# Decode attention with a gated MLP: x loaded as 16 rows, the last values in two halves, 76 first key rows

## The chip, the cores and the metric

The kernel runs on one core of a Trainium2 chip. The metric is the device time of one execution in microseconds (us). A core has a matrix engine (PE, its weight loads shown apart as PEld), a vector engine (DVE), a scalar engine (ACT), GpSimd (POOL) and SyncE (SP), which here only issues transfers. ACT and SP each have a queue of transfers; all transfers run on the same 16 DMA engines. Matmuls read SBUF and write PSUM.

## The reference

One token, x of 512 values. It is normalised (xn), and goes two ways: through attention over the last 4096 positions of a cache of 32 heads, and through a small MLP. The results are multiplied and added to x.

```
xn = layernorm(x)
q = (xn @ wq) in 32 heads of 128
k, v = the last 4096 rows of k_cache, v_cache of each head      # bf16, 32 MiB each
s = softmax(q k^T / sqrt(128)) v, all heads side by side, @ wo  # wo: 4096 x 512
h = gelu(layernorm(xn) @ w1); hs = shift(h) @ w2                # S = 1: the shifted h is zero
x1 = xn + hs
g = silu(x1 + gelu(layernorm(x1) @ w3) @ w4)
out = x + s * g
```

With a sequence of one position, the shifts by one and two positions leave only padding, so the kernel multiplies w2 by a column of zeros (`shifted_bf`) and doesn't load w1.

## The kernel before

**Groups.** The 32 heads are taken in 8 groups of 4 (G = 4, NG = 8). Keys of a group are one tile of 128 partitions by 128 rows ("chunks", CP = 128) of 128 values, 4 MiB; partition p holds 128 neighbouring positions of one head (32 partitions a head). Values lie the same way. The K tiles have three buffers and the V tiles two (K_BUFS, V_BUFS), and the V buffers take the place of the first weights (pool `wts`), once those have been used.

**Loads.** All but x and wq are issued by SP, in program order (`load`, L75): w2, w3, w4, then K0 in two halves, K1, K2, V0, K3, V1 and so on, with pieces of wo between them; at the end V7 in three pieces (`cuts`, L528: chunks 0 to 64, 64 to 96, 96 to 128), and four rows of wo of 128 x 512, two by two (L544). A buffer's next load waits for the engines that read the buffer, and what stands behind it in SP's queue waits too. ACT issues x twice and wq (L78 to L85): as 128 partitions of four values (`x_bf`, from which the statistics and q are made) and as four rows of 128 values on partitions 0, 32, 64 and 96 (`x_row`, for the end), after POOL has cleared that tile.

**Start.** The statistics of x (`ln_stats`), the product with wq in rows (L208), copies of q for DVE (`q_bc`) and for PE (`q_pair`), and the MLP (L245 to L280), whose result g_row waits for the end. This part is in an order that a scheduler makes; from L529 on the order of PE, DVE and ACT is the program's own.

**Scores.** The keys' rows of a group are shared out. For the first nd(g) rows of each partition (L308: 64 for group 0 and from LATE = 7 on, else 80) DVE multiplies by q and sums over 128 values (`k_vector`, L321 and L323), in four steps of nd/4 rows. The others go to PE: transposes of pairs of rows (`k_turn`, L339), a copy by ACT (L342), and two matmuls per pair (`k_scores`, L350), in batches of up to eight rows; `sm_own` (L359) takes the right head's part. `sm_max`, `sm_turn`, `sm_exp`, `sm_den`, `sm_rden` make the softmax. In round s of the loop (L533) the scores of group s are made, the softmax of group s-1, and the values of group s-2 (LAG = 2).

**Values.** `v_wide` (L427) multiplies four chunks by the probabilities of four chunks at a time, 16 rows into the sum `ov`; `v_turn` transposes it, `v_add` (L450) takes the fitting parts together to `oT`, and `v_out` (L471) multiplies by 1/denominator to `o`. For the last group the first 96 chunks go that way; `v_add` writes its result over a PSUM tile that `v_open` has opened, and `v_part` (L461) then adds the last 32 chunks to that tile one by one with the values as weights, so that nothing has to be turned.

**End.** `ox_spread` and `ox_pick` turn blocks of o for the wide products with wo (`y_wide`, L520), summed over four partitions by `rows_add` (L155). The last four heads go head by head (`y_head`, `rows_add`): four matmuls each with one row of wo into y_ps. Then y = y_ps * g_row, out_row = y + x_row (L654, L656), and the store. `warm(n)` (L509) issues n matmuls of zeros that no one reads.

`small.tile([P, 96], BF16, name="pad")` at L71 is not used by anything: it only moves what lies behind it.

Of the kernel before, what the change touches and what calls it, by code (L numbers as in the profile page):

```python
# [18 lines left out]
G = 4  # L19
# [3 lines left out]
LATE = 7  # L23
# [3 lines left out]
def kernel(  # L27
# [24 lines left out]
    CP = G * W // P  # L52
    PB = P // G
# [14 lines left out]
    ps_o = ctx.enter_context(tc.tile_pool(name="ps_o", bufs=1, space=PSUM))  # L68
    ps_y = ctx.enter_context(tc.tile_pool(name="ps_y", bufs=1, space=PSUM))
    sm_pool = ctx.enter_context(tc.tile_pool(name="sm", bufs=3))  # L70
    small.tile([P, 96], BF16, name="pad")  # L71
    wts_guard = tc.tile_pool(name="wts", bufs=1)
    wts = wts_guard.__enter__()

    def load(dst, src):  # L75
        return tc.keep_in_program_order(nc.sync.dma_start(out=dst, in_=src))  # L76

    x_bf = small.tile([P, KC], BF16, name="x_bf")  # L78
    nc.scalar.dma_start(out=x_bf[:], in_=A_x.rearrange("a b (p c) -> p (a b c)", p=P))
    x_row = small.tile([P, P], BF16, name="x_row")  # L80
    nc.gpsimd.memset(x_row[:], 0.0)
    nc.scalar.dma_start(out=x_row[0:P:32, :], in_=A_x.rearrange("a b (j n) -> (a b j) n", j=KC))
    wq_sb = wts.tile([P, KC, HD], BF16, name="wq_sb")
    nc.scalar.dma_start(out=wq_sb[:].rearrange("p c n -> p (c n)"),
                        in_=A_wq.rearrange("(a b c) n -> b a (c n)", a=4, c=KC))  # L85
# [93 lines left out]
        return xc, negmean, rstd  # L179


    x_f = small.tile([P, KC], FP32, name="x_f")
    nc.vector.tensor_copy(out=x_f[:], in_=x_bf[:])
    xc, negmean, rstd = ln_stats(x_f[:], "x")
    xn_f = small.tile([P, KC], FP32, name="xn_f")
    nc.vector.tensor_scalar(out=xn_f[:], in0=xc[:], scalar1=rstd[:], scalar2=None, op0=ALU.mult)
# [51 lines left out]
    z3_bf = small.tile([P, KC], BF16, name="z3_bf")  # L238
    nc.vector.tensor_scalar(out=z3_bf[:], in0=xc3[:], scalar1=rstd3[:], scalar2=None, op0=ALU.mult)

    xn_row = small.tile([P, P], FP32, name="xn_row")
    nc.vector.tensor_scalar(out=xn_row[:], in0=x_row[:], scalar1=negmean[:], scalar2=rstd[:],
                            op0=ALU.add, op1=ALU.mult)
# [62 lines left out]
    st = {}  # L306

    def nd(g):  # L308
        return 64 if g == 0 or g >= LATE else 80

    def k_open(g):
        st[g] = {
# [132 lines left out]

    def v_add(g):
        s = st[g]
        if g < NG - 1:
            s["oT"] = sm_pool.tile([P, G], FP32, tag="oT", name="oT")
        nc.vector.tensor_reduce(out=s["oT"][:], in_=s["ot"][:].rearrange("p (x m) -> p m x", m=32)[:, 0:G, :],  # L450
                                axis=AX.X, op=ALU.add)

    def v_open(g):
        st[g]["oT"] = ps_tr.tile([P, G], FP32, tag="pt", name="oT")
        nc.tensor.matmul(st[g]["oT"][:], lhsT=zero_bf[:], rhs=zero_bf[:, 0:G], start=True, stop=False,
                         skip_group_check=True)

    def v_part(g, v, c0, c1):
        s = st[g]
        for c in range(c0, c1):  # L460
            nc.tensor.matmul(s["oT"][:], lhsT=v[:, c, :], rhs=s["pT"][:, c, :], start=False,  # L461
                             stop=(c == CP - 1), skip_group_check=True)

    def v_out(g):
        h = G * g
        b = [i for i, (h0, _) in enumerate(blocks) if h >= h0][-1]
        if b not in o_blk:
            o_blk[b] = sm_pool.tile([P, blocks[b][1]], BF16, tag=f"o{b}", bufs=1, name="o")
        c = h - blocks[b][0]
        if g >= NG - 5:  # L470
            nc.vector.tensor_tensor(out=o_blk[b][:, c:c + G], in0=st[g]["oT"][:], in1=st[g]["rden"][:],  # L471
                                    op=ALU.mult)
            return
        for k in range(G):
            nc.scalar.mul(o_blk[b][:, c + k:c + k + 1], st[g]["oT"][:, k:k + 1], st[g]["rden"][:, k:k + 1])
# [49 lines left out]
        rows_add(y_ps, o_blk[3][:, h - h_part:h - h_part + 1], wo_row(h), h == H - 1)  # L525

    NG = H // G
    cuts = (0, 64, 96, CP)  # L528
    region = tc.manual_schedule(engines={mybir.EngineType.PE, mybir.EngineType.DVE,  # L529
                                         mybir.EngineType.Activation})  # L530
    region.__enter__()
# [1 line left out]
    for s in range(NG + LAG):  # L533
# [7 lines left out]
            wo_rows = v_pool.tile([P, H - h_part, D], BF16, tag="wo_rows", bufs=1, name="wo_rows")  # L541
        if last:
            v = load_kv(v_pool, A_v_cache, h, cuts)
            for r in (H - G, H - 2):  # L544
                load_rows(r, 2)
        elif h >= 0:
            v = load_kv(v_pool, A_v_cache, h)
        if h == 3:
# [71 lines left out]
        elif s == NG:  # L620
            ox_pick(1)
            sm_turn(NG - 1)
            sm_exp(NG - 1)
            y_wide(1, False)
            sm_den(NG - 2)
            sm_rden(NG - 2)
            y_wide(0, False)
            warm(3)
            v_wide(h, v)
            sm_den(NG - 1)  # L630
            sm_rden(NG - 1)
            v_turn(h)
            v_add(h)
            v_out(h)
            ox_spread(2)
        else:
            v_open(h)
            warm(2)
            v_wide(h, v, cuts[1], last=False)
            ox_pick(2, 1)  # L640
            y_wide(2, True)
            nc.scalar.copy(out=y_sum[:], in_=yr[0][:].rearrange("p j n -> p (j n)"))
            v_wide(h, v, cuts[2], cuts[1])
            warm(2)
            v_turn(h)
            v_add(h)
            rows_add(y_ps, ind, y_sum, False)
            v_part(h, v, cuts[2], CP)
            v_out(h)
            for r in range(H - G, H):  # L650
                y_head(r)
# [36 lines left out]
```

## Time and profile before

| | us |
|---|---|
| median of 3 runs | 193.54 (193.43 to 193.62) |
| the profiled execution | 193.37 |
| its span, first to last instruction | 191.2 |
| x_bf issued, landed | 0.74, 4.76 |
| first DVE work on K0 | 25.93 |
| K1 landed | 41.98 |
| last values landed | 186.19 |
| store issued | 188.71 |

Bytes moved: 79.02 MB, 413 GB/s over the span. Busy shares of the span: PE 63%, DVE 79%, ACT 47%, POOL 1%.

The profile is that of one execution. Its page gives for each engine the busy time, 40 slices of the span, the transfer queues, the chain of work that ended last (followed back from the last instruction to what released it), and the costliest groups of instructions. A line L461 is line 461 of the program. The trace behind it can be asked for the busy time in any window, for the timeline, and holds a record of every packet (queue, start, length, size) and of each completion by each DMA engine. "Granted clock" is the share of PE's full clock that its throttle allowed.

### The profile page before, as it was taken

To read this page: it belongs to the slowest core of one execution; us is meant where nothing else is said; L and a number is where in the kernel's file an instruction comes from. 1 tells how busy PE (TensorE), PEld (TensorE's weight loads), DVE (VectorE), ACT (ScalarE), POOL (GpSimd) and SP (SyncE) were. 2 spreads that over 40 slices of the span, in tenths; PEclk is the share of its full clock that TensorE was granted. 3 is DMA by queue.
4 is the path that set the end of the run, shared out by engine and by line. 5 is a ranking of instruction groups with operands and counts; after the bars stand their busy time and mean duration, and the time that the engine had idled before them with its cause. 6 is when DMAs were issued, how large, how long until landed. Compare 5 with 4: busy or idle time off the path is not lost.

```text
span 191.2 us, 2843 instructions
## 1 busy us (share of the span) xinstructions
PE 121.2 (63%) x1161; PEld 77.0 (40%) x1161; DVE 150.9 (79%) x175; ACT 89.5 (47%) x191; POOL 2.4 (1%) x11
## 2 busy tenths in 40 slices
PE   1554853989826368356945773681889289749772
PEld 0430222767615334243434432540764078513321
DVE  1560169979999999999999999999999997990111
ACT  2001270887795076527364654552575147743120
POOL 2110000000000000000000000000000000000000
PEclk9999696555665556955585579558555855996999
DMA  6999999999999999999999999999999998999990
GB/s 202 436 444 410 431 425 432 439 439 437 432 440 432 432 428 439 439 439 418 428 418 425 439 428 408 456 432 435 439 439 434 428 432 379 471 435 394 415 372 29
DMA packets 4572, 79.02 MB, mean 413 GB/s; under 512 B 624, under 2 KB 1232, under 8 KB 1488
## 3 DMA queue, kind: packets, MB, share of 16 engines
q1 hardware_dynamic: 4264, 74.65, 91.6%
q10 hardware_dynamic: 296, 4.20, 5.1%
q8 instruction: 9, 0.15, 0.3%
q14 instruction: 3, 0.02, 0.0%
HBM read 78.84 MB, written 0.00 MB: 412 GB/s over the span
## 4 chain that ended last, share of the span: by engine, by line
DVE 47%; DMA 42%; PE 6%; ACT 1%; issue 1%; SPq 1%; DVEq 0%; ACTq 0%
DMA kv<-in_A_k_cache_dram 31%; DVE S L323 28%; DVE prod L321 16%; DMA kv<-in_A_v_cache_dram 9%; PE pt L339 3%; DMA x_bf<-in_A_x_dram 2%; ACT kt L342 1%; PE ov L427 1%; PE sT L350 1%; DVE m L366 1%; SPq L76 1%; DVE S L364 1%; DVE mx L374 1%; PE oT L461 1%; PE ot_ps L444 0%
## 5 line engine op out<-in xcount | busy, mean ns | idle before, releaser
L323 DVE TENSOR_REDUCE S<-prod 128x20 f32<-128x2560 bf16 (+1 forms) x32 | 86.0, 2686 | 1.1
L342 ACT COPY kt<-pt 128x1024 bf16<-128x1024 bf16 x52 | 51.4, 1013 | 40.0 <-PE pt L339 38.1
L339 PE MATMUL pt<-ident_f,kv 128*128 128x128 f32 x208 | 49.2, 392 | 10.0 <-DMA kv<-in_A_k_cache_dram 10.0
L321 DVE TENSOR_TENSOR prod<-kv,q_bc 128x2560 bf16<-128x2560 bf16 (+1 forms) x32 | 45.4, 1417 | 3.6 <-ACT q_pair L225 1.8
L339 PEld LDWEIGHTS pt<-ident_f,kv 128*128 128x128 f32 x208 | 36.2, 205 | 13.9 <-DMA kv<-in_A_k_cache_dram 9.3
L350 PE MATMUL sT<-q_pair,kt 128*128 128x8 bf16 x416 | 19.6, 170 | 14.9 <-ACT kt L342 14.8
L350 PEld LDWEIGHTS <-kt 128*128 128x128 bf16 x416 | 16.9, 105 | 26.1 <-ACT kt L342 24.9
L427 PE MATMUL ov<-kv,pT 128*16 128x512 bf16 x248 | 23.2, 536 | 1.2 <-DMA kv<-in_A_v_cache_dram 1.2
L388 ACT ACTIVATE pT<-S,mb 128x128 bf16<-128x128 f32 x32 | 13.9, 572 | 0.3
L372 PE MATMUL mt_ps<-ident_f,m 128*1 128x128 f32 x8 | 2.9, 360 | 16.6 <-DVE rden L399 16.1
L433 ACT COPY ov_sb<-ov 128x512 f32<-128x512 f32 x8 | 4.7, 586 | 18.4 <-PE ov L427 18.4
L427 PEld LDWEIGHTS <-pT 128*16 128x16 bf16 x248 | 6.9, 112 | 14.3 <-issue 12.7
L359 ACT ACTIVATE own<-sT,par 128x48 f32<-128x48 f32 (+1 forms) x32 | 7.5, 356 | 3.7 <-PE sT L350 3.7
L444 PE MATMUL ot_ps<-ident_f,ov_sb 128*128 128x128 f32 x32 | 7.5, 379 | 2.2 <-ACT mb L384 1.7
L211 DVE CAST q_row<-qr_ps 128x512 bf16<-128x512 f32 x1 | 0.7, 692 | 10.0 <-PE qr_ps L208 10.0
L388 ACT ACTIVATION_READ_ACCUMULATOR pT<-S,mb 128x1 f32 x32 | 8.3, 258 | 0.0
L372 PEld LDWEIGHTS mt_ps<-ident_f,m 128*1 128x1 f32 x8 | 0.6, 80 | 17.1 <-DVE rden L399 16.4
L399 DVE RECIPROCAL rden<-den_ps 128x4 f32<-128x4 f32 x8 | 1.4, 175 | 6.7 <-PE den_ps L394 6.7
L381 PE MATMUL mb_ps<-md,par_t 5*128 5x4 f32 x16 | 3.9, 311 | 4.1 <-DVE md L376 4.1
L255 ACT ACTIVATE a_row<-a_ps 128x384 bf16<-128x384 f32 x1 | 0.5, 491 | 12.1 <-remote 12.1
L444 PEld LDWEIGHTS ot_ps<-ident_f,ov_sb 128*128 128x128 f32 x32 | 4.8, 188 | 3.2 <-ACT mb L384 2.1
L208 PE MATMUL qr_ps<-wq_sb,xq_bf 128*1 128x512 bf16 x32 | 3.5, 611 | 3.6 <-DMA wq_sb<-in_A_wq_dram 3.6
(122 smaller groups left out, 82.8 us busy)
## 6 DMA issues: line engine op xcount, KB each, us to landing
kv<-in_A_k_cache_dram SPq DMA_DIRECT2D x7, 4096.0 KB, 31.0
kv<-in_A_v_cache_dram SPq DMA_DIRECT2D x7, 4096.0 KB, 30.6
wq_sb<-in_A_wq_dram ACTq DMA_DIRECT2D x1, 4096.0 KB, 17.5
kv<-in_A_k_cache_dram SPq DMA_DIRECT2D x2, 2048.0 KB, 27.5
wo<-in_A_wo_dram SPq DMA_DIRECT2D x1, 2048.0 KB
kv<-in_A_v_cache_dram SPq DMA_DIRECT2D x1, 2048.0 KB
kv<-in_A_v_cache_dram SPq DMA_DIRECT2D x2, 1024.0 KB, 16.3
w_sb<-in_B_w_dram SPq DMA_DIRECT2D x1, 1376.0 KB, 10.3
```

The lines of the kernel that those rows point to most:

```text
L208: nc.tensor.matmul(qr[b][32 * a:32 * a + 1], lhsT=xq_bf[:, c:c + 1], rhs=wc[:, 4 * b:4 * b + 4, a, :], start=False, stop=(c == KC - 1), sk ...
L321: nc.vector.tensor_tensor(out=prod[:, 0:m, :], in0=kn[:, rows, :], in1=q_bc[:, g:g + 1, :].to_broadcast([P, m, Dh]), op=ALU.mult)
L323: nc.vector.tensor_reduce(out=st[g]["S"][:, rows], in_=prod[:, 0:m, :], axis=AX.X, op=ALU.add)
L339: nc.tensor.transpose(pt[:, i, :], kn[:, c:c + 2, :].rearrange("p c d -> p (c d)").bitcast(FP32), ident_f[:])
L342: nc.scalar.copy(out=kts[b][:, 0:n, :], in_=pt[:, 0:n, :].bitcast(BF16))
L350: nc.tensor.matmul(st[g]["sT"][:, c:c + 2, :].rearrange("p c a -> p (c a)"), lhsT=kt[:, i, l::2], rhs=q_pair[:, g, l, :], start=(l == 0), ...
L359: nc.scalar.mul(s["own"][:, 0:m, a], s["sT"][:, 0:m, a], par[:, a:a + 1])
L381: nc.tensor.matmul(mb_ps[:], lhsT=par_t[:].rearrange("k b a -> k (b a)"), rhs=md[:], start=True, stop=True)
L388: nc.scalar.activation(out=s["pT"][:, :, a], in_=s["S"][:], func=ACT.Exp, scale=scale, bias=mb[:, a:a + 1], accum_out=s["sum"][:, a:a + 1])
L427: nc.tensor.matmul(ov[r:r + 4 * G], lhsT=s["pT"][:, c:c + 4, :].rearrange("p i a -> p (i a)"), rhs=v[:, c:c + 4, :], start=(i < 4), stop=( ...
L433: nc.scalar.copy(out=s["ov_sb"][:], in_=ov[:])
L444: nc.tensor.transpose(ot_ps[:, step * j:step * j + P], s["ov_sb"][:, j, :], ident_f[:])
```

## The change

1. x is loaded once, as 16 rows of 32 values (`x_in`). The column form is made by a matmul that copies each row to 8 partitions (`x_up`), a product with a mask that keeps each partition's own four values (`x_own`), and a sum. The row form `x_row` is made by a second matmul from `x_in` spread over four blocks (`r_in`, `r_up`).
2. nd(0) is 76 instead of 64: 12 rows of each partition of group 0 go from PE to DVE. Its 52 PE rows are 7 batches instead of 8.
3. The last values come in four pieces instead of three (cuts at 64, 96, 112). `v_part` gets a PSUM tile of its own (`oP`), apart from the sum of the first 96 chunks (`oT`, now in SBUF), so it waits for `v_open` alone; a new DVE instruction adds the two (`both`). On PE the sum of the wide products (`rows_add` of `y_sum`) and the first 16 of the 32 chunks now stand ahead of `v_turn`, and two `warm` matmuls are gone.
4. The last four rows of wo are loaded as three and one instead of two and two.
5. The unused tile at the start grows from 96 to 208 values per partition and a second one of 112 is added, as other small tiles came and went.

As the scheduler of the first part has new instructions to place, their order there changes as well: the mask reductions (`make_masks`) stand between the steps of the statistics, and four of the 20 matmuls with w3, and the Gelu behind them on ACT, come after the matmuls with wq.

```diff
-    small.tile([P, 96], BF16, name="pad")
+    small.tile([P, 208], BF16, name="pad")
...
-    x_bf = small.tile([P, KC], BF16, name="x_bf")
-    nc.scalar.dma_start(out=x_bf[:], in_=A_x.rearrange("a b (p c) -> p (a b c)", p=P))
-    x_row = small.tile([P, P], BF16, name="x_row")
-    nc.gpsimd.memset(x_row[:], 0.0)
-    nc.scalar.dma_start(out=x_row[0:P:32, :], in_=A_x.rearrange("a b (j n) -> (a b j) n", j=KC))
+    XR, XC = 16, D // 16
+    x_in = small.tile([XR, XC], BF16, name="x_in")
+    nc.scalar.dma_start(out=x_in[:], in_=A_x.rearrange("a b (r n) -> (a b r) n", r=XR))
...
+    m8 = P // XR
+    x_up = wts.tile([XR, XR, m8], BF16, name="x_up")
+    nc.vector.tensor_copy(out=x_up[:], in_=ident_bf[0:XR, 0:XR].unsqueeze(2).to_broadcast([XR, XR, m8]))
+    x_own = wts.tile([P, m8], BF16, name="x_own")
+    nc.vector.tensor_reduce(out=x_own[:], in_=ident_bf[:].rearrange("d (i t) -> d t i", t=m8), axis=AX.X, op=ALU.max)
+    x_all = ps_misc.tile([P, m8, KC], FP32, tag="misc", name="x_all")
+    nc.tensor.matmul(x_all[:].rearrange("p t c -> p (t c)"), lhsT=x_up[:].rearrange("k r t -> k (r t)"), rhs=x_in[:],
+                     start=True, stop=True)
+    x_pick = wts.tile([P, m8, KC], FP32, name="x_pick")
+    nc.vector.tensor_tensor(out=x_pick[:], in0=x_all[:], in1=x_own[:].unsqueeze(2).to_broadcast([P, m8, KC]), op=ALU.mult)
     x_f = small.tile([P, KC], FP32, name="x_f")
-    nc.vector.tensor_copy(out=x_f[:], in_=x_bf[:])
+    nc.vector.tensor_reduce(out=x_f[:], in_=x_pick[:].rearrange("p t c -> p c t"), axis=AX.X, op=ALU.add)
...
+    r_slot = wts.tile([XR, KC], BF16, name="r_slot")
...
+    r_in = wts.tile([XR, KC, XC], BF16, name="r_in")
+    nc.vector.tensor_tensor(out=r_in[:], in0=x_in[:].unsqueeze(1).to_broadcast([XR, KC, XC]),
+                            in1=r_slot[:].unsqueeze(2).to_broadcast([XR, KC, XC]), op=ALU.mult)
+    xr_ps = ps_misc.tile([P, P], FP32, tag="misc", name="xr_ps")
+    nc.tensor.matmul(xr_ps[:], lhsT=r_up[:].rearrange("k j b -> k (j b)"), rhs=r_in[:].rearrange("k a n -> k (a n)"),
+                     start=True, stop=True)
+    x_row = small.tile([P, P], BF16, name="x_row")
+    nc.vector.tensor_copy(out=x_row[:], in_=xr_ps[:])
...
     def nd(g):
-        return 64 if g == 0 or g >= LATE else 80
+        return 76 if g == 0 else 64 if g >= LATE else 80
...
     def v_add(g):
         s = st[g]
-        if g < NG - 1:
-            s["oT"] = sm_pool.tile([P, G], FP32, tag="oT", name="oT")
+        s["oT"] = sm_pool.tile([P, G], FP32, tag="oT", name="oT")
...
     def v_open(g):
-        st[g]["oT"] = ps_tr.tile([P, G], FP32, tag="pt", name="oT")
-        nc.tensor.matmul(st[g]["oT"][:], lhsT=zero_bf[:], rhs=zero_bf[:, 0:G], start=True, stop=False,
+        st[g]["oP"] = ps_tr.tile([P, G], FP32, tag="pt", name="oP")
+        nc.tensor.matmul(st[g]["oP"][:], lhsT=zero_bf[:], rhs=zero_bf[:, 0:G], start=True, stop=False,
                          skip_group_check=True)
...
-            nc.tensor.matmul(s["oT"][:], lhsT=v[:, c, :], rhs=s["pT"][:, c, :], start=False,
+            nc.tensor.matmul(s["oP"][:], lhsT=v[:, c, :], rhs=s["pT"][:, c, :], start=False,
...
+        if g == NG - 1:
+            sm_pool.tile([P, 112], BF16, tag="pad", bufs=1, name="pad")
+            both = sm_pool.tile([P, G], FP32, tag="both", bufs=1, name="both")
+            nc.vector.tensor_tensor(out=both[:], in0=st[g]["oP"][:], in1=st[g]["oT"][:], op=ALU.add)
+            st[g]["oT"] = both
...
-    cuts = (0, 64, 96, CP)
+    cuts = (0, 64, 96, 112, CP)
...
             v = load_kv(v_pool, A_v_cache, h, cuts)
-            for r in (H - G, H - 2):
-                load_rows(r, 2)
+            load_rows(H - G, G - 1)
+            load_rows(H - 1, 1)
...
             v_wide(h, v, cuts[2], cuts[1])
-            warm(2)
+            rows_add(y_ps, ind, y_sum, False)
+            v_part(h, v, cuts[2], cuts[3])
             v_turn(h)
             v_add(h)
-            rows_add(y_ps, ind, y_sum, False)
-            v_part(h, v, cuts[2], CP)
+            v_part(h, v, cuts[3], CP)
             v_out(h)
```

More of the change, by code (lines that the diff above doesn't have):

```diff
@@ L239 @@
     nc.vector.tensor_scalar(out=z3_bf[:], in0=xc3[:], scalar1=rstd3[:], scalar2=None, op0=ALU.mult)
+    r_slot = wts.tile([XR, KC], BF16, name="r_slot")
+    nc.vector.tensor_reduce(out=r_slot[:], in_=ident_bf[0:XR, 0:XR].rearrange("k (j a) -> k a j", a=KC), axis=AX.X, op=ALU.max)
+    r_row = wts.tile([XR, KC], BF16, name="r_row")
+    nc.vector.tensor_reduce(out=r_row[:], in_=ident_bf[0:XR, 0:XR].rearrange("k (j a) -> k j a", a=KC), axis=AX.X, op=ALU.max)
+    r_up = wts.tile([XR, KC, PB], BF16, name="r_up")
+    nc.vector.tensor_copy(out=r_up[:], in_=r_row[:].unsqueeze(2).to_broadcast([XR, KC, PB]))
+    r_in = wts.tile([XR, KC, XC], BF16, name="r_in")
[6 more added lines that the diff above has]
+    nc.vector.tensor_copy(out=x_row[:], in_=xr_ps[:])
     xn_row = small.tile([P, P], FP32, name="xn_row")
```

## The prediction

> **What bounds the kernel now.** I read the page first (shares, slices, queues), then the chain of waits, then DMA rates by window, then the timeline of the last 5 us.
>
> ```profile
> span 191.2 us, 2843 instructions
> ...
> PE 121.2 (63%) x1161; PEld 77.0 (40%) x1161; DVE 150.9 (79%) x175; ACT 89.5 (47%) x191; POOL 2.4 (1%) x11
> ...
> DMA  6999999999999999999999999999999998999990
> ...
> q8 instruction: 9, 0.15, 0.3%
> ```
>
> ```profile
> 2.70:186.20 183.50, 119.08 (x1112) 75.79 (x1112) 149.66 (x166) 89.45 (x191) 1.11 (x2) 0.69 1.00 429
> ...
> 185.25:185.50 0.25, 0.25 (x4) 0.24 (x3) 0.00 (x0) 0.00 (x0) 0.00 (x0) 1.00 0.81 316
> 186.00:186.25 0.25, 0.07 (x5) 0.02 (x2) 0.00 (x0) 0.00 (x0) 0.00 (x0) 1.00 0.67 238
> ```
>
> The second block is windows; its last two columns are the DMA engines' busy share and GB/s. From 2.7 us to 186.2 us the engines are busy for 1.00 of the time at 429 GB/s: one unbroken stream of 79.02 MB. DVE is busy for 79% and looks like a rival bound, but it can only matter if it lets the stream run dry or is late for the end. So the time is: start of the stream, bytes over rate, and what follows the last bytes.
>
> ```profile
> 130.42 23.05 DMA kv<-in_A_k_cache_dram
> ...
> 168.94 17.25 DMA kv<-in_A_v_cache_dram
> ...
> 186.24 0.97 PE oT L461 x32
> ...
> 187.23 0.17 DVE o L471
> ...
> 187.45 0.59 PE y_ps L155 x16
> ...
> 188.06 0.30 DVE y L654
> ```
>
> The chain of waits (start, length, what) says the same: the last transfers were queued 23 and 17 us before they landed. After the last values land at 186.19 come 32 small matmuls, one DVE product, 16 row matmuls, two DVE operations and the store. One thing more is in the view of the tile wo_rows and in the timeline from 187.75 us on:
>
> ```profile
> L76 SPq DMA_DIRECT2D wo_rows<-in_A_wo_dram x2: 469/531/593, 169.6 to 170.2; - x2
> ...
> DMA to landing us min/median/max: 17.3/17.4/17.5
> ```
>
> ```profile
> 187.73 0.28 PE L155 MATMUL y_ps<-wo_rows,o 128*1 128x128 bf16 x8
> ```
>
> The second wo_rows transfer, issued at 170.2, lands 17.5 us later: 187.69 in the trace's completion records. The last eight row matmuls start at 187.73, not right behind the first eight. So **two chains meet at the end**: values, oT, o; and the last weight rows. Shortening one gains only up to the other.
>
> The completion records also show how uneven the end is. Each transfer is finished by 16 DMA engines one by one: the last wo_rows from 185.55 to 187.45, and one straggler at 187.69. The packet records name the cause: nine 16 KB instruction loads (queue q8), each 0.95 to 1.3 us long on one engine, and the data packet behind each some 0.5 us longer than usual. Each makes one engine some 1.6 us late, a different one each time. The ninth starts at 187.21, under the last wo_rows transfer, and makes the straggler.
>
> **The change, part by part.**
>
> *x as 16 rows.* Two transfers (128 packets of 8 B, 4 rows of 256 B) become one. In the records an 8 B packet takes 9 ns, so 8 per engine are 0.07 us; while they interleave with w2 (2.8 to 3.4 us) the stream runs at 328 to 349 GB/s against 412 for bare 4 KB packets (159 ns each on 16 engines): (412-342)/412 x 0.6 us = 0.10 us. I take **-0.10**, bounds -0.16 and 0. ACT's x_row issue (1.09 us) goes, so wq is issued at about 1.2 instead of 2.29; that reorders the stream (wq lands earlier, w3 and w4 later), its length stays. SP's K0b issue loses its wait for x_bf (1.3 us), with w2 to w4 already queued behind it: nothing. Added: three DVE operations and a matmul ahead of the statistics, six DVE operations and a matmul for x_row. None has a row of its own; small DVE rows here are 0.15 to 0.38 us, a small matmul 0.16 to 0.6. In the built program the mask reductions now also sit between the statistics. In all 2 to 3 us, against x landing up to 1.5 us earlier: xq_bf is ready between 8.4 and 12 us instead of 9.05. Cover: the q matmuls wait for wq until 19.87 (18.8 if wq gains all of 1.1 us); past that cover each microsecond would delay K group 0. Four of the 20 w3 matmuls and the Gelu now stand behind the q matmuls, so ACT does a table load (1.28) and the Gelu (0.49) before the q copies: q_bc ends at 25.2 to 26.1 instead of 25.36. K0's first half lands at 25.83, so DVE starts at most 0.3 us later.
>
> *76 first rows.* Rows per step go from 16 to 19. Between the rows for 16 (1.22 and 2.29 us) and 20 (1.49 and 2.82): 1.42 and 2.69, +0.60 a step, **+2.4 us on DVE**; PE and ACT lose one batch of eight (1.1 us). DVE sat idle for 1.32 us before K1 (42.08), so it is now 1.1 to 1.4 us late there. What is late next: the release of K buffers. K7 is issued at up to 131.8 instead of 130.42, but its bytes only begin when V4 has landed (143.75): 12 us of cover. K7's DVE work has a 1.15 us idle gap at 162.58 that takes up most of the rest, and the exponentials of the last group end at 174.5, 6.8 us before the first values land (181.31). Zero; 1.4 us if that cover were gone.
>
> *Pads.* In both programs values and weights lie at multiples of 256 bytes (values 160000 and 160512), the K buffers 128 beside one. Nothing moves: zero. That it can matter is in the landings: a K transfer takes 9.71 us, a V transfer of the same size 9.66.
>
> *Last values.* The last 32 chunks become 16 and 16, 4 KB packets instead of 8 KB: 2 x 159 against 309 ns, 8 per engine: **+0.07** (bounds 0 and 0.15). With x that cancels, and the last values still land near 186.19. The issue of a further transfer (0.55 us on SP) lies 6 us ahead of the stream's need. Behind them 16 matmuls: spacing (0.97-0.165)/31 = 26 ns, so 0.55 us, end 186.79. The new sum "both" costs what the 4-wide product costs, 0.16 and about 0.04 around it; then o, to 187.2; row matmuls from 187.25 instead of 187.45. The first 16 chunks (185.0 to 185.55), the transposes (0.66, to 186.2) and the reduction (0.23, to 186.5) end before the 186.8 at which "both" could start. The chain of values alone would gain 0.20 to 0.23.
>
> A rule against this split: the Trainium skill, "DMA: Bandwidth & Descriptors", section "Bandwidth", says to batch transfers to at least 1 MiB for 75% of peak. Here the 1 MiB piece before the rows landed 2.46 us after the one before it, 426 GB/s, since transfers queue behind each other; by the rule each half would be below three quarters of that rate, an estimate of 1.6 us instead of 1.2 for each and 0.8 in the sum.
>
> *Rows three and one.* The last transfer holds one row, so four matmuls (about 0.25) instead of eight (0.28) follow the last byte: 0.03. The stream's end is what counts: 187.69 with the straggler, 187.45 without. The page counts 2 x 1161 PE instructions for nine loads, one per 258. The change takes out 12 transposes, 24 score matmuls and two warm matmuls and adds two: 36, so 72 instructions with their weight loads. The ninth load, which came with some 32 instructions to go, is then past the end. So the rows land at 187.45, row matmuls end at max(187.25+0.28, 187.45+0.04)+0.25 = 187.78 instead of 188.04. **Tail -0.24**, bounds -0.28 and -0.03.
>
> Sum: -0.10+0.07-0.24 = -0.27, of which I keep -0.24, as x's rate loss is read from 0.6 us of start-up. The profiled execution took 193.37 us (2.17 outside the span), 0.17 under the median; 193.37-0.24 = 193.13, and at the median 193.54-0.24 = **193.3**.
>
> **The rivals.** Measurements here tell a difference from none at about 0.2%, 0.39 us.
>
> 1. *The straggler stays* (18%): the ninth load still falls on the last rows, or another does. Rows land at 187.69, matmuls end at 187.98: -0.06, **193.5**. For it: loads come at any time in the trace. Against: the count above.
>
> 2. *The stream also starts earlier* (25%): 128 descriptors of x_bf leave the moment w2 is issued (both at 0.73), and w2's first packets start at 1.78. If they had held w2 back, up to the 0.40 us of x_bf's issue comes on top: **192.9**. Against: w2's issue, 0.39 us, is the shortest of SP's loads.
>
> 3. *The clock falls in the tail* (8%), **slower**. Two warm matmuls (0.60 us at 184.3) go. Windows (PE busy first, granted clock third from the end):
>
> ```profile
> 170.00:171.00 1.00, 0.20 (x1) 0.10 (x1) 0.92 (x5) 0.12 (x2) 0.00 (x0) 1.00 0.82 344
> 171.00:172.00 1.00, 0.27 (x1) 0.08 (x1) 0.88 (x4) 0.00 (x0) 0.00 (x0) 1.00 1.09 459
> 172.00:173.00 1.00, 0.57 (x10) 0.40 (x10) 0.24 (x2) 0.16 (x1) 0.00 (x0) 1.00 0.91 393
> 174.00:175.00 1.00, 1.00 (x16) 0.17 (x7) 0.00 (x0) 0.75 (x4) 0.00 (x0) 0.50 1.11 475
> ```
>
> After 3 us at about 0.35 the clock was halved; at 0.65 (180 to 184) it held. At half clock the transposes take 1.11 us instead of 0.66 and the small matmuls up to twice. Then first half to 185.9, transposes to 187.0, second half to 187.55 to 187.95, sum and product to 188.35 at most, rows to 188.6 to 189.2: +0.5 to +1.2, **194.0 to 194.7**. It decides from a busy share of about a third over the last 3.4 us; with 0.61+0.40+0.55+0.66 us of work from 183.8 to 186.2 I expect 0.75. The Trainium skill, "TensorE: Matmul & The Clock Gate", Part 1, has the clock fall after an idle window of some 3.4 us; by that rule nothing falls here, but the rows above show a fall without one.
>
> 4. *Cover gone* (4%): DVE's 1.4 us, a load that hits an engine already late (1.6), or a start paid by the added transfer as by the lone store (issued 188.71, landed 190.38: 1.67) reaches the end: 194.7 to 195. Against: the 6 to 12 us above, and pieces that land 2.46 us apart. (That last form is where the rule on batching would show; the trace speaks against it.)
>
> **How the numbers follow.** The forecast has 45%, its own range 193.1 to 193.5; a quarter of it lies beyond -0.2% (193.15). Faster: 0.11 + 0.25 = 0.36. Same: 0.34 + 0.18 = 0.52. Slower: 0.12. The range reaches to rival 2 with its bounds and just short of the clock's fall: 192.8 to 193.9.
>
> **What would show it.** Right: the last-stage timeline has row matmuls starting near 187.25 and ending near 187.8, "both" at 186.8, the ninth instruction load after the last row's landing or missing, clock 1.0 to the end, the stream at 429 GB/s. DVE idle before K1 gone. Wrong: a landing of the last row at 187.7 (rival 1); first data before 1.6 us (rival 2); any break of the stream after 2.7 us, or values later than 186.3, would break the frame itself.

## The result, and the profile after

| | before | after |
|---|---|---|
| median of 6 runs, us | 193.36 (193.17 to 193.62) | 192.72 (192.51 to 192.91) |
| ratio after/before, 95% interval | | 0.9965 (0.9955 to 0.9975) |
| the profiled execution | 193.37 | 192.51 |
| its span | 191.2 | 190.7 |
| outside the span | 2.16 | 1.79 |
| last values landed | 186.19 | 185.91 |
| last row of wo landed | 187.69 | 187.25 |
| y starts | 188.06 | 187.57 |
| store issued | 188.71 | 188.21 |

The change is 0.64 us faster, just under the low end of the range that was given (192.8), and more than the 0.24 that the steps added up to. The two columns already show the point of this case: of the 0.86 us between the two profiled executions 0.49 lie in the span, and 0.37 lie outside it, where the prediction carried a constant.

The page of the changed kernel:

```profile
span 190.7 us, 2819 instructions
...
PE 119.6 (63%) x1143; PEld 74.9 (39%) x1143; DVE 154.9 (81%) x184; ACT 89.0 (47%) x191; POOL 2.2 (1%) x10
...
DMA  5999999999999999999999999999999998999991
...
q8 instruction: 9, 0.15, 0.3%
q14 instruction: 4, 0.03, 0.0%
```

DVE has 4.0 us more work and nine more instructions, PE 1.6 us less. The stream of transfers is as full as before. There are still nine instruction loads on q8, and a fourth one on q14, which matters below.

Windows of the same run (PE busy and PEld, DVE, ACT, POOL; then granted clock, DMA share, GB/s):

```profile
2.70:185.90 183.20, 117.72 (x1109) 73.93 (x1108) 152.31 (x169) 88.14 (x191) 1.11 (x2) 0.68 1.00 430
...
174.00:175.00 1.00, 1.00 (x13) 0.41 (x17) 0.18 (x1) 0.65 (x4) 0.00 (x0) 0.50 1.15 492
178.00:179.00 1.00, 1.00 (x25) 0.39 (x20) 0.00 (x0) 0.00 (x0) 0.00 (x0) 1.00 0.96 410
...
185.00:186.00 1.00, 0.82 (x17) 0.58 (x14) 0.18 (x1) 0.00 (x0) 0.00 (x0) 1.00 0.74 269
```

The stream is unbroken from 2.7 us to the last values at 430 GB/s, and the clock is at 1.00 when the tail begins. The end of its chain of waits (start, length, what):

```profile
170.02 15.90 DMA kv<-in_A_v_cache_dram
...
185.96 0.57 PE oP L482 x16
...
186.55 0.17 DVE both L494
...
186.75 0.17 DVE o L497
...
186.97 0.58 PE y_ps L153 x16
...
187.57 0.30 DVE y L680
```

From the last landing to y it is 1.66 us (185.91 to 187.57) against 1.87 before (186.19 to 188.06). 16 matmuls stand behind the last values instead of 32, and the sixteen row matmuls run in one go: their last row landed at 187.25, while they ran.

### The profile page after: what moved, and what is told of

It reads as the page before. It is cut to its first block, busy times and chain, and to the rows that moved or that the text cites. A ratio compares the mean times of both kernels' runs of the same rounds, so it can differ in the third digit from the quotient of the medians.

```text
span 190.7 us, 2819 instructions
## 1 busy us (share of the span) xinstructions
PE 119.6 (63%) x1143; PEld 74.9 (39%) x1143; DVE 154.9 (81%) x184; ACT 89.0 (47%) x191; POOL 2.2 (1%) x10
## 4 chain that ended last, share of the span: by engine, by line
DVE 71%; DMA 20%; PE 3%; SPq 2%; issue 1%; ACT 1%; DVEq 0%; ACTq 0%
DVE S L345 43%; DVE prod L343 22%; DMA kv<-in_A_k_cache_dram 12%; DMA kv<-in_A_v_cache_dram 8%; SPq L76 2%; PE ov L449 2%; DVE m L388 1%; DVE S L386 1%; ACT kt L364 1%; DVE mx L396 1%; DVE md L398 0%; DVE oT L471 0%; DVE hr L295 0%; DVE ox L524 0%; PE y_ps L153 0%
## 5 line engine op out<-in xcount | busy, mean ns | idle before, releaser
L345 DVE TENSOR_REDUCE S<-prod 128x20 f32<-128x2560 bf16 (+2 forms) x32 | 87.6, 2736 | 1.1
L364 ACT COPY kt<-pt 128x1024 bf16<-128x1024 bf16 (+1 forms) x51 | 49.7, 1004 | 43.9 <-PE pt L361 42.7
L361 PE MATMUL pt<-ident_f,kv 128*128 128x128 f32 x202 | 46.1, 381 | 7.4 <-DMA kv<-in_A_k_cache_dram 7.4
L343 DVE TENSOR_TENSOR prod<-kv,q_bc 128x2560 bf16<-128x2560 bf16 (+2 forms) x32 | 46.1, 1442 | 3.3 <-DMA kv<-in_A_k_cache_dram 3.1
L361 PEld LDWEIGHTS pt<-ident_f,kv 128*128 128x128 f32 x202 | 34.0, 199 | 11.3 <-DMA kv<-in_A_k_cache_dram 8.7
L372 PE MATMUL sT<-q_pair,kt 128*128 128x8 bf16 x404 | 19.0, 170 | 16.2 <-ACT kt L364 16.0
L372 PEld LDWEIGHTS <-kt 128*128 128x128 bf16 x404 | 16.2, 105 | 26.5 <-ACT kt L364 25.5
L449 PE MATMUL ov<-kv,pT 128*16 128x512 bf16 x248 | 24.4, 561 | 0.4 <-DMA kv<-in_A_v_cache_dram 0.4
L381 ACT ACTIVATE own<-sT,par 128x48 f32<-128x48 f32 (+2 forms) x32 | 7.5, 352 | 3.7 <-PE sT L372 3.7
L403 PEld LDWEIGHTS mb_ps<-md,par_t 5*128 5x128 f32 x16 | 3.8, 293 | 6.9 <-PE sT L372 5.6
```

What stands on the lines that cost most here:

```text
L343: nc.vector.tensor_tensor(out=prod[:, 0:m, :], in0=kn[:, rows, :], in1=q_bc[:, g:g + 1, :].to_broadcast([P, m, Dh]), op=ALU.mult)
L345: nc.vector.tensor_reduce(out=st[g]["S"][:, rows], in_=prod[:, 0:m, :], axis=AX.X, op=ALU.add)
L361: nc.tensor.transpose(pt[:, i, :], kn[:, c:c + 2, :].rearrange("p c d -> p (c d)").bitcast(FP32), ident_f[:])
L364: nc.scalar.copy(out=kts[b][:, 0:n, :], in_=pt[:, 0:n, :].bitcast(BF16))
L372: nc.tensor.matmul(st[g]["sT"][:, c:c + 2, :].rearrange("p c a -> p (c a)"), lhsT=kt[:, i, l::2], rhs=q_pair[:, g, l, :], start=(l == 0), ...
L381: nc.scalar.mul(s["own"][:, 0:m, a], s["sT"][:, 0:m, a], par[:, a:a + 1])
```

## The experiments

All times are medians; "outside" is the median of device time minus span over a kernel's runs, which is 2.15 to 2.18 for every set of runs of the kernel before, beside a span of 191.2. All ratios are to the kernel before on the same chip.

**Each part alone.** e1 has the new loading of x (part 1 of the change), e2 the split of the values, the separate sum and the rows three and one (parts 3 and 4), e3 the 76 rows (part 2). In e1 and e2 the unused tile at the start is sized so that every large buffer keeps its place relative to 256 bytes; e3 changes one number alone.

```diff
 # e1
-    small.tile([P, 96], BF16, name="pad")
+    small.tile([P, 80], BF16, name="pad")
-    x_bf = small.tile([P, KC], BF16, name="x_bf")
...
+    x_in = small.tile([XR, XC], BF16, name="x_in")
...
 # e2
-    cuts = (0, 64, 96, CP)
+    cuts = (0, 64, 96, 112, CP)
...
-            for r in (H - G, H - 2):
-                load_rows(r, 2)
+            load_rows(H - G, G - 1)
+            load_rows(H - 1, 1)
...
 # e3
-        return 64 if g == 0 or g >= LATE else 80
+        return 76 if g == 0 else 64 if g >= LATE else 80
```

Expected of e1:

> The kernel before with x as 16 rows alone (column and row form made by matmuls; unused tile 80 instead of 96 values, so that weights and values stay at the addresses of before). Theory A (the x transfers cost the stream: 144 small packets made the 16 DMA engines start unevenly, and the last engine decides): last values land near 185.9 instead of 186.19, the 16 completions of a value transfer spread over 1.75 us instead of 1.95, time -0.2 to -0.35 us. Theory B (the 0.28 us at the landing come from the 76 rows, which move the instruction loads against the stream): time within 0.08 us of before, spread 1.95.

Expected of e2:

> The kernel before with the end alone: values in four pieces, the sum of the last 32 chunks in a PSUM tile of its own, rows three and one, no warm matmuls in the last stage; addresses of weights and values as before. Both theories: the values land at 186.15 to 186.3 with a spread of 1.95 us, the row matmuls end 0.2 to 0.25 us earlier against that landing, time -0.15 to -0.25 us. If the last row's landing (straggler) still binds: 0 to -0.08 us, row matmuls waiting for it at 187.7.

Expected of e3:

> The kernel before with 76 instead of 64 first rows in group 0 alone. Theory A: no change, within 0.08 us, DVE reaches K1 1.1 to 1.4 us late and nothing else moves. Theory B: -0.2 to -0.35 us, the spread of the completions near 1.75 us.

| | time | ratio (95%) | span | outside |
|---|---|---|---|---|
| e1, x alone | 193.73 | 1.0021 (1.0012 to 1.0030) | 191.9 | 1.79 |
| e2, tail alone | 193.24 | 0.9993 (0.9985 to 1.0002) | 191.3 | 1.87 |
| e3, 76 rows alone | 193.31 | 1.0002 (0.9986 to 1.0019) | 191.5 | 1.81 |

The parts do not add up to the whole: +0.34, -0.15 and about 0 against -0.64. Neither theory of e1 had a place for a slower kernel; the intervals of e2 and e3 take in no change at all. And in all three the time outside the span is lower by 0.3 to 0.4, although e3 changes one number. Two questions follow: what hides the parts' gains, and what the time outside hangs on.

What hides them can be read in the profiled executions, one for each kernel. The chain of waits of e2's ends with the rows, not with the values:

```profile
172.98 14.75 DMA wo_rows<-in_A_wo_dram
...
187.78 0.26 PE y_ps L155 x4
```

The records of packets show a q8 instruction load at 187.32 (0.95 us), under the last row; one engine lands the row at 187.73, the other fifteen by 187.55. Twelve row matmuls run from 187.34, the last four wait. This is the straggler of the prediction's first rival, met by half of the change, not by the whole. In e1's, y starts at 187.73, 0.33 us before the kernel before, and the store is issued at 188.38, 0.33 earlier as well. But the store's last completion is at 190.87 instead of 190.38: the others come by 190.04, and a q14 instruction load of 8 KB runs from 189.52 for 0.37 us. (The packet records carry no number of the engine; that a load and a late completion share one is read from their times.) What was won is lost while the store is on its way.

For e3 the profiled execution was one of its long ones, 194.29 (its runs reach from 192.82 to 194.36). Windows (columns as above) and the end of its chain:

```profile
175.00:178.00 3.00, 3.00 (x24) 1.04 (x21) 0.18 (x1) 1.33 (x8) 0.00 (x0) 0.50 0.93 393
178.00:180.00 2.00, 2.00 (x15) 0.51 (x17) 0.00 (x0) 0.00 (x0) 0.00 (x0) 0.50 0.90 377
180.00:181.00 1.00, 1.00 (x16) 0.37 (x12) 0.00 (x0) 0.00 (x0) 0.00 (x0) 0.66 0.97 410
```

```profile
185.50 0.59 ACT y_sum L642
...
186.63 0.66 PE ot_ps L444 x4
187.29 0.33 PE y_ps L155 x8
187.62 0.95 PE oT L461 x32
```

The kernel before has, in the first of these stretches:

```profile
175.00:178.00 3.00, 3.00 (x31) 0.82 (x31) 0.00 (x0) 0.00 (x0) 0.00 (x0) 0.66 0.91 388
```

PE works without a gap from 173.8, at half clock until 180.7; in the kernel before, half clock ended at 177.1. Its backlog then reaches the end: the 32 small matmuls start at 187.62, 1.4 us after the values have landed (186.25). So in this execution, with 76 rows and a late clock, the end is over a microsecond late; in the median e3 costs nothing. That the 76 rows are what makes such executions more frequent is not shown: three of e3's twelve runs lie above 194 us and none of the kernel before, but f1 (below), with 64 rows, has long runs too. The Trainium skill, "TensorE: Matmul & The Clock Gate", Part 1, has the full clock come after at least one busy window of 3.4 us, and has these windows run free of the program. Here it took two in e3 (half clock from 173.86 to 180.69) and one in the kernel before (173.65 to 177.06), with PE busy throughout both: within that rule, which doesn't say which of the two will come.

**The instruction load under the store.** If e1 loses to the position of a load, a program with a little more DVE code should move it. e7 is e1 with two more memsets of one value that nobody reads; e8 is the kernel before with ten.

```diff
+    idle = const.tile([P, 2], FP32, name="idle")
...
             if s == 3:
+                for _ in range(2):
+                    nc.vector.memset(idle[0:1, 0:1], 0.0)
```

> e1_x (x as 16 rows alone) with two 1-element DVE memsets added in round 3, which nobody reads. In e1_x an 8 KB instruction load of queue q14 starts at 189.52 us, under the output store (188.38), whose last completion comes at 190.87 instead of some 190.05. Theory L (DVE's longer program reaches the next block of instructions just at the end, and the load delays the store): with two more instructions the load comes earlier, the store completes within 1.7 us of its issue, and the time falls by 0.5 to 0.8 us against e1_x, to 192.9 to 193.25. If the load isn't the cause: as e1_x, 193.7.

> The kernel before with ten 1-element DVE memsets in round 3 that nobody reads (0.06 us each on an engine that is not the bound), so that DVE's program is as long as that of e1_x. Theory L: a load of queue q14 now falls on the last 2 us, the store completes 0.4 to 0.9 us later, time +0.3 to +0.8 us against an unchanged copy. If DVE's length doesn't matter: as the unchanged copy, within 0.1 us.

e7 took 192.90 (0.9983, 0.9974 to 0.9991), 0.83 us less than e1 by two more instructions (0.73 by the ratios, as the two ran on different chips): its fourth q14 load stands at 173.92, far ahead of the store. Span 191.1. e8 took 193.89 (1.0033, 1.0022 to 1.0044): its load is at 189.77 (0.50 us), under the store that was issued at 188.63, and the store's last completion comes at 191.27, the others by 190.30. The transfers of e8 from 189.4 us on, when nothing but the store should be left:

```profile
DMA packets 9, 0.01 MB, mean 4 GB/s; under 512 B 8, under 2 KB 8, under 8 KB 8
...
q14 instruction: 1, 0.01, 1.5%
q1 hardware_dynamic: 8, 0.00, 0.3%
```

Eight small packets of the store, and one instruction packet with five times their time. So the position of one load is worth 0.5 to 0.9 us: the store's completion is that much later with the load under it (e1, e8), and the time fell by 0.7 to 0.8 when it moved away (e7). In the changed kernel the fourth q14 load comes at 187.26, after the last row and before the store: nothing waits for it.

**x and the tail together**, the changed kernel with 64 first rows:

```diff
-        return 76 if g == 0 else 64 if g >= LATE else 80
+        return 64 if g == 0 or g >= LATE else 80
```

> The changed kernel with 64 first rows in group 0 again (x and the end stay changed). Theory C (the gain is x and the end together, and 76 rows do nothing): within 0.1 us of the changed kernel, 192.6 to 192.8, span 190.8. Theory D (the three parts are needed together, since 76 rows move the PE's instruction loads): the last row lands late again, 0.2 to 0.4 us slower than the changed kernel.

192.80 (0.9973, 0.9962 to 0.9983), span 190.9, outside 1.81. As theory C has it, the 76 rows do about nothing between e6 and the whole. With e7 this gives a size to the parts inside the span once no load spoils them: x 191.2 to 191.1, that is -0.1 (e7), x and tail -0.3 (e6), so the tail -0.2. These are at the edge of what the runs can tell: medians of the span are given to 0.1 us, and e7's ratio (0.9983) is no lower than that of o2 below (0.9980), which has nothing of x.

**The time outside the span.** c0 is the kernel before, measured as if it were a change. o2 is the kernel before with one unread DVE memset (the edit of e8, once instead of ten times); g1 the same memset on POOL. g4 is the changed kernel with eleven small preparing operations moved from DVE to POOL, which brings DVE's program back to the length that it had before.

```diff
 # g1
+                nc.gpsimd.memset(idle[0:1, 0:1], 0.0)
...
 # g4
-    nc.vector.memset(q_pair[:], 0.0)
+    nc.gpsimd.memset(q_pair[:], 0.0)
...
-    nc.vector.tensor_copy(out=r_up[:], in_=r_row[:].unsqueeze(2).to_broadcast([XR, KC, PB]))
+    nc.gpsimd.tensor_copy(out=r_up[:], in_=r_row[:].unsqueeze(2).to_broadcast([XR, KC, PB]))
...
```

> The kernel before, unchanged, measured as if it were a change. In all runs so far the time outside the span is 2.18 us for the kernel before and 1.8 to 1.87 us for every other kernel, even for one that differs in a single constant. Theory M (the difference belongs to the way of measuring): this copy too has 1.85 us outside its span and a time 0.3 us below that of before, ratio 0.9983 to 0.9988. Theory P (it belongs to the programs): 2.18 us and ratio 1.000.

> The kernel before with one 1-element DVE memset more in round 3, that nobody reads. Theory N (the 0.35 us outside the span hang on the length of DVE's program, 186 instructions in before and 187 or more in all others): 1.8 us outside the span, span as before (191.1 to 191.2), time 0.3 to 0.4 us below before. If it isn't DVE's length: 2.17 us outside, ratio 1.000.

> The kernel before with one memset of two unread values more, on GpSimd instead of the vector engine. Theory N (the time outside the span hangs on the length of the vector engine's program): outside 2.17 us as in the kernel before, 193.4 in all. Rival (any change of the program, or of its whole length, does it): outside 1.8, 193.0.

> The changed kernel with eleven of its small preparing operations (memsets, copies of masks, the spread of x for the row form) done by GpSimd, so that the vector engine runs fewer instructions than in the kernel before. Theory N: outside the span 2.17 instead of 1.8, span as in the changed kernel (190.7 to 190.9), 192.9 to 193.1 in all. Rival (the time outside hangs on something else that the change has, such as the lone small load of x): 1.8 and 192.5 to 192.7.

| | DVE instructions in the built program | time | ratio (95%) | span | outside |
|---|---|---|---|---|---|
| before | 186 | 193.38 | 1 | 191.2 | 2.16 |
| c0, the same | 186 | 193.38 | 1.0002 (0.9993 to 1.0011) | 191.2 | 2.18 |
| g1, one more on POOL | 186 | 193.28 | 1.0001 (0.9992 to 1.0010) | 191.1 | 2.16 |
| o2, one more on DVE | 187 | 193.00 | 0.9980 (0.9970 to 0.9989) | 191.2 | 1.80 |
| e3, 76 rows | 187 | 193.31 | 1.0002 (0.9986 to 1.0019) | 191.5 | 1.81 |
| after, second time (g2) | 199 | 192.82 | 0.9977 (0.9967 to 0.9986) | 191.0 | 1.83 |
| g4, after with less on DVE | 186 | 193.19 | 0.9995 (0.9983 to 1.0007) | 191.0 | 2.18 |

The count takes in DVE's waits and branches, which is how e3, with the same 175 busy instructions as before, comes to 187; the traces hold two fewer of each program (184 for before, 185 for e3 and o2, 197 for after). One memset that nobody reads makes the kernel 0.38 us faster without moving its span; 0.36 of it lie outside. The same memset on another engine does nothing. And the changed kernel loses 0.37 us when its DVE program is cut back to 186, with its span unchanged:

```profile
span 191.0 us, 2820 instructions
...
PE 122.8 (64%) x1143; PEld 77.4 (41%) x1143; DVE 153.8 (81%) x173; ACT 89.2 (47%) x191; POOL 4.4 (2%) x21
...
q14 instruction: 3, 0.02, 0.0%
```

So 0.33 us of the change's gain hang on DVE's program having more than 186 instructions. It holds for every program of this study: those with 186 (before and its copy c0, g1, g4, and e5 below) have 2.15 to 2.18 us outside, twelve with 187 to 199 have 1.77 to 1.87. g4 also says what is left of the change when this is taken away: 193.19 against 193.37 of the kernel before on the same chip, a ratio of 0.9995 whose interval takes in no change.

The profile's views end with the span, but the trace's records of semaphore updates go on, and show where the difference lies. In all 19 traces updates follow the last instruction for 1.7 to 1.8 us; then comes a pause, and then the last four. The pause is 0.47 us in the five traces of programs with 186 and 0.10 to 0.11 us in the fourteen others, which is the 0.36 us. So the difference is spent after the program's end, not ahead of the span. What is waited for in the pause the traces don't name, and whether shorter programs than 186 would gain or lose was not tried.

**Alignment.** e4 is the changed kernel with K buffers moved from 128 beside a multiple of 256 bytes to a multiple, e5 the kernel before with values and weights moved 128 bytes off.

```diff
 # e4
+    lead = ctx.enter_context(tc.tile_pool(name="lead", bufs=1))
+    lead.tile([P, 64], BF16, name="lead")
...
-    small.tile([P, 208], BF16, name="pad")
+    small.tile([P, 144], BF16, name="pad")
...
 # e5
-    small.tile([P, 96], BF16, name="pad")
+    small.tile([P, 160], BF16, name="pad")
```

> The changed kernel with a leading unused tile of 128 bytes, so that the K buffers too lie at multiples of 256 bytes (values and weights stay where the change has them). If the address decides the 0.05 us by which a K transfer (9.71 us) takes longer than a V transfer (9.66): all 4 MiB transfers take 9.66, the last values land 0.35 to 0.4 us earlier than in the changed kernel, time 192.35 (ratio to before 0.9945). If it is the order or the source: no difference from the changed kernel, 192.7.

> The kernel before with its unused tile 128 bytes longer, so that weights and value buffers lie 128 beside a multiple of 256 bytes, as its K buffers do; not one instruction more or less. If the address makes the 0.05 us by which each 4 MiB K transfer is slower than a value transfer: value transfers take 9.71 us instead of 9.66, the first DMA engine finishes the last values 0.3 to 0.45 us later (184.7 instead of 184.3), time +0.3 to +0.45 us inside the span. Outside the span: 2.17 us if the number of instructions decides the 0.35 us found there, 1.8 if any other program has it.

e5 took 194.06 (1.0036, 1.0024 to 1.0048), span 191.9: +0.7 us by 128 bytes, more than the 0.3 to 0.45 that were expected. Nine transfers of 4 MiB, from the first completion of K1's predecessor at 30 us to 118 us, take 86.95 us with everything aligned (e4), 87.17 with K beside (before and after alike), 87.42 with all beside (e5): about 0.05 us, half a per cent, for each unaligned transfer. Single executions scatter: the other aligned ones (f1, h1, g3 and f2 below) take 87.05, 87.03, 86.94 and 87.23, the last no less than the 87.14 to 87.24 of those with K beside. But in all five aligned executions the last values land at 185.75 to 185.89, and in all others at 185.91 or later. The Trainium skill, "DMA: Bandwidth & Descriptors", section "How a descriptor splits into AXI transactions", lets a descriptor that doesn't start at a multiple of 256 bytes read from the boundary below; for 4 KB packets that is an estimate of 132 beats for 128, 3%. The direction agrees; here, where the address in question is the one that is written, the size is a sixth of it.

e4 took 192.68 (0.9975, 0.9962 to 0.9987) beside 192.72 and 192.82 of the changed kernel, not the 192.35 that was expected. The first DMA engine ends the values at 183.85 instead of 184.19, but the last only at 185.75 instead of 185.91, and then PE is late: half clock until 178.2, the second half of the last chunks' matmuls ends at 186.7, and y starts at 187.60 (187.57 in the changed kernel). The bytes came earlier and nobody was ready for them.

**Taking that further.** f1 is e4 with 64 first rows; f2 is e4 without the three dummy matmuls `warm(3)` that stand ahead of the last values on PE; g3 is f2 again, on one chip with g2. h1 is the kernel before, with its K buffers aligned and one unread DVE memset, and nothing of the change.

```diff
 # f2, against e4
-            warm(3)
...
 # h1, against the kernel before
+    lead.tile([P, 64], BF16, name="lead")
...
+                nc.vector.memset(idle[0:1, 0:1], 0.0)
```

> The changed kernel with aligned K buffers (as e4_kalign) and 64 first rows in group 0. e4_kalign let the stream end 0.16 to 0.34 us earlier, but PE came late: it ran at half clock until 178.2 and held the last stage. Theory E (76 rows made DVE, and so the last softmax and PE, later than they need be): with 64 rows PE waits for values again, time 192.45 to 192.6, no run above 193. If the clock alone decides: as e4_kalign, 192.7 with a few runs at 193.2 to 193.4.

> e4_kalign without the three warm matmuls ahead of the values of group 6 (0.6 to 1.46 us of PE time in which PE is late when its clock is halved). Theory F (in the last 15 us PE's chain is as long as the stream): PE is ready 0.6 to 1.4 us earlier and waits for values, time 192.4 to 192.55. If the three kept the clock up: the clock stays at half for another 3.4 us and the time is 0.3 us or more above e4_kalign.

> The changed kernel once more, on the same chip as the others of this call: 192.7, between 192.5 and 192.9.

> The changed kernel with the K buffers at multiples of 256 bytes and without the three dummy matmuls ahead of the last value pieces, once more. If its gain is real, 0.2 to 0.3 us below the changed kernel on the same chip: 192.4. If it was the luck of few runs: 192.7.

> The kernel before with a 128-byte tile ahead of the K buffers (K, values and weights all at multiples of 256 bytes) and one memset of two unread values on the vector engine. My theory: outside the span 1.8 instead of 2.17; the last values' first DMA engine done 0.3 us earlier than in the kernel before (183.9 instead of 184.2), so a span of 190.9 to 191.1 and 192.7 to 192.9 in all, as much as the whole change. Rival (the end is bound by PE's work or by an instruction load there, so that earlier values gain nothing): span 191.2, 193.0.

| | time | ratio (95%) | span | outside |
|---|---|---|---|---|
| f1 | 192.55 (192.31 to 193.56) | 0.9966 (0.9952 to 0.9980) | 190.75 | 1.81 |
| f2 | 192.42 (192.29 to 193.13) | 0.9957 (0.9942 to 0.9971) | 190.65 | 1.79 |
| g3 (f2 again) | 192.48 (192.35 to 192.57) | 0.9956 (0.9944 to 0.9968) | 190.7 | 1.77 |
| h1 | 192.65 (192.63 to 192.74) | 0.9964 (0.9951 to 0.9978) | 190.9 | 1.82 |

f2 beats both kernels: all five runs of g3 lie below all of g2 (192.66 to 193.76) on the same chip, 0.34 us apart in the median. How much of that is the missing dummy matmuls is not shown: g3 has the alignment as well, and the intervals of f2 and e4, which differ in the dummies alone, overlap. That they were in the way of real ones fits two executions: in g2's the three take 1.39 us at half clock (176.99 to 178.38), and g3's is fast (192.57) though its half clock lasts until 180.2, nearly as long as in e3's long one. Of f1, theory E failed: it said no run above 193, and three of twelve lie at 193.15 to 193.56, with 64 rows, so long runs come without the 76 rows too. What makes them stays open, as the profiled execution was a short one. The end of h1's chain:

```profile
169.52 16.37 DMA kv<-in_A_v_cache_dram
...
185.94 0.97 PE oT L464 x32
...
186.93 0.17 DVE o L474
...
187.15 0.54 PE y_ps L157 x16
```

It has the old tail, 32 matmuls behind the last values, but these land at 185.89 instead of 186.19. So 128 bytes of nothing and one memset of nothing give as much (-0.69 us) as the whole change (-0.64 and -0.55). Against o2, which has the memset alone, the span is 0.3 shorter.

## Why the prediction was off, point by point

- **What bounds the kernel: right.** Stream of 429 to 430 GB/s from 2.7 us to the last values, and the tail behind them, in both kernels. e5 shows it from the other side: 0.5% on some of the transfers is in the end time. That the values land at 185.91 instead of 186.19 (186.08 in g2) is no clear gain: in c0, g1 and o2, which load x as before, they land at 186.02 to 186.33.
- **x, -0.10: not refuted, and too small to be shown.** e7 has -0.1 in the span, o2's time is as low without x. The cover of the added operations held: in the trace K0's first half lands at 25.56 and DVE starts on it at 25.65, against 25.83 and 25.93. It was not seen that 10 more DVE instructions also move instruction loads, which makes x alone slower (e1).
- **76 rows, nothing: right in the median.** DVE's idle time of 1.32 us before K1 is gone, as said; the step from K0 to K1 in the timeline of the changed kernel's DVE:

```profile
40.20 2.69 DVE L345 TENSOR_REDUCE S<-prod 128x19 f32<-128x2432 bf16 x1
42.92 1.49 DVE L343 TENSOR_TENSOR prod<-kv,q_bc 128x2560 bf16<-128x2560 bf16 x1
```

  The 12 us of cover for K7 held too. What was not seen is that PE has little room ahead of the last values: in e3's long execution, at half clock until 180.7, it came over a microsecond late.
- **Pads, nothing: right** for what the change does; the 0.05 us that the prediction read from the landings is a lever that the change leaves unused (h1).
- **Split values and the separate sum, -0.20 to 0.23 from the landing to y: right**, 1.66 against 1.87 us.
- **Rows three and one: the time right, the reason wrong, so that part was luck.** The count that put the ninth instruction load past the end (one per 258 PE instructions) failed: it came at 186.74. The count was also twice too high: 12 rows are six pairs, so 6 transposes and 12 score matmuls go, and the pages have 1143 matmuls for 1161, 18 fewer and not 36. The load did no harm: all sixteen parts of the last row had landed by 187.25, none of them late, so the engine that it fell on must have been done with its own (seven were by 186.5). In e2 the same load at 187.32 fell on that row.
- **The sum inside the span: right in size, as far as it can be told.** -0.24 was predicted; the spans of the two sets of the changed kernel's runs have medians of 190.8 and 191.0 against 191.2, that is -0.4 and -0.2.
- **The step that failed is the term that was not in the sum:** "193.37 us (2.17 outside the span)" was carried over as a constant. It is 1.84 in the changed kernel, 0.33 less, about half of the whole gain. o2 and g4 show it on either side: one more DVE instruction takes it from the kernel before, and a DVE program of 186 gives it back to the changed one. With it the same sum gives 193.37 - 0.24 - 0.33 = 192.8, against 192.72 and 192.82 measured. The forecast of 193.3 was further off by its base: it stood on a median of three runs, 193.54, where six have 193.36.
- **The rivals.** The straggler (193.5) took the tail alone, not the whole. An earlier stream, which came nearest in time (192.9), did not happen: the first bytes move at 2.03 us in the profiled execution of the changed kernel and at 1.75 in g2's, against 1.78 before. That the measured time lies near 192.9 is a coincidence. The clock did not fall in the tail; it came back at 177.7 instead of 177.1. The rule that the prediction made for its fall (a busy share of about a third) is not what the records show: in the 3.41 us ahead of the fall at 173.65 PE was busy for 0.50 of the time, over all traces such windows reach 0.81, and windows at 0.51 held the clock. No cover was gone in the median.

## What to carry to other kernels

Before predicting a change of half a microsecond, look at what lies outside the span and under the last transfers: one instruction more, of no use, moved this kernel by -0.38 us, and an instruction load that slid under the last store made it 0.5 to 0.9 later. To learn what a part of a change is worth, compare spans and look where the instruction loads fell, and run the whole against a version with padding instructions only; the difference that is left is the change's own. Here little is left: 0.9965 and 0.9977 for the whole against 0.9980 for one unread memset. And in a kernel that is bound by its transfers, try every large buffer at a multiple of 256 bytes: it was worth 0.3 us of span in h1 against o2, and nothing in e4, where PE was late.

## What the runs showed of the hardware

- The time outside the profiled span is not the same for all programs: 2.15 to 2.18 us with 186 DVE instructions in the program, 1.77 to 1.87 with 187 to 199; an instruction on POOL has no such effect. The difference is one pause in the semaphore updates after the program's end, 0.47 us against 0.10 to 0.11; its cause stays open.
- Instruction loads share the DMA engines with the data: 16 KB take 0.9 to 1.3 us on one engine (q8), 8 KB 0.31 to 0.53 us (q14), and data can land late by them: the last completion of the store by 0.8 and 1.0 us behind the others (e1, e8), that of the last row by 0.2 (e2).
- A 4 MiB load into a buffer that lies 128 bytes beside a multiple of 256 takes some 0.05 us longer than 9.66 us (nine of them 87.42 us in e5, 86.95 in e4; one aligned execution, f2's, took 87.23 all the same).
